# Reworking the first 100 microseconds of a fused Fourier-filter and gated-FFN kernel, and the places of its side work

## The chip, the cores and the metric

The kernel runs on one core of one Trainium2 chip. A core has a matrix engine (PE; PEld is its weight load), a vector engine (DVE), an activation engine (ACT), a GpSimd engine (POOL), and SyncE (SP), which here only issues DMAs. Each engine takes its instructions strictly in program order. DMAs are issued from the queues of SP, ACT and POOL; all of them move their data with the same 16 DMA engines. On-chip data lies in SBUF, matmul results in PSUM.

The metric is the device time of one execution in microseconds. The kernel before has a median of 905.79 us over 10 runs (904.47 to 909.28).

## The reference

`x` has 8 batches of 3,008 tokens with 256 features. Each batch is filtered in frequency space along the tokens, and each filtered token then goes through a gated feed-forward network with 1,536 hidden features.

```python
X = np.fft.rfft(x, axis=1)                      # x: (8, 3008, 256), float32
F = (filt_r + 1j * filt_i)[None, :, :]          # (1505, 256)
y = np.fft.irfft(X * F, n=3008, axis=1)
x2 = y.reshape(24064, 256)
gate = np.maximum(x2 @ w_gate, 0.0)             # w_gate, w_val: (256, 1536)
out = (gate * (x2 @ w_val)) @ w_out             # w_out: (1536, 256)
```

## The kernel before

**Stages.** 3,008 = 94 x 32, so the transform is done as a 94-point and a 32-point part. Per batch there are three stages, all matmuls against small tables.
- Stage A is the 94-point transform. It reads `x` and stores its result to `Abuf` in HBM, from where `at` is loaded with another layout (the exchange goes through HBM). It exists in two forms. The plain form (`items_a`, 16 items, float32 matmuls of 512 columns, L276) is used for batches 0 and 1. The folded form is used from batch 2 on: `load_chunk` loads a quarter of a batch into `XP[j]`, `fold_chunk` adds and subtracts mirrored rows (six tensor_tensor instructions on POOL, L308 to L313), and `tiled_a` does 32 small matmuls (L322), evicts with ACT and DVE (L329) and stores.
- Stage B has six steps per batch. `fwd` (L363) is the 32-point transform into two PSUM tiles `psX`. `product` multiplies them by the real filter `Ftr` and the imaginary filter `Fti` (DVE, L379; in batch 0 some go to POOL by way of a copy `xs` on ACT, L376/L377, chosen by `POOL_U`). `inv` (L393) transforms back, ACT evicts (`dsb`, L400), and SP stores to `Dbuf`.
- Stage C (`item_c`, L448) loads `dC` from `Dbuf`, does the inverse 94-point part and leaves the transposed tokens `yT` of a block of 512: half h=0 is evicted by ACT (L453), half h=1 by DVE (L455).

**The main stream.** 47 blocks of 512 tokens, 12 steps each. A step is `gv` (two matmuls into `psV`, two into `psG`, L464; ACT turns `psV` into `vsb`, L467; DVE makes `prod` = max(psG, 0) * vsb, L469) and `o_part` of the block before (four matmuls into `psO`, L483; output evicted by ACT, L489, at steps 5 and 11). Block 0 has no `o_part` beside it.

**Order.** The order on each engine is the program order, written out by hand. `at_step(s, f)` hangs side work behind step s of the stream (s counts from the first step of block 0): Stages A and B of the next batches, loads, and so on. `end` is the step from which a batch is needed. PSUM is handed out by four tags of two tiles each (`fft`, `psv`, `psg`, `pso`); a tag's tiles are used in turn, and a tile is free when its last reader is done.

**The prologue** runs before the stream: batch 0's `x` and the tables are loaded by SP, the filters by POOL (`load_filters`, after a small copy, `hold_gpsimd`, that waits for the first part of `x`; then `load_own_filters`, the last rows). `warm(n)` issues n matmuls on a constant tile to keep PE busy. `items_a(0)` runs with `warm(1, 256)` or `make_back_t` between its items; `make_back_t`, `make_back_u` build the back-transform tables `I2t`, `I2u` from `F2` (PE, then DVE or ACT); `place_filter` copies filter rows across partitions (L238, DVE, one on ACT). `first_b` is Stage B of batch 0; its `amid` runs items of Stage A of batch 1 between its steps, and the rest of them follow. The loads of `x` of batch 1 wait on SP behind `gate`, a small DMA that reads `at`. The second halves of the gate and value weights (`load_vg`) and the output weight (`load_o`) are issued by POOL after a small load of the end of `Dbuf0`.

Of the kernel before, what the change touches and what calls it, by code (L numbers as in the profile page):

```python
# [12 lines left out]
FP32 = mybir.dt.float32  # L13
# [17 lines left out]
NROW = 96  # L31
# [89 lines left out]
def kernel(  # L121
# [32 lines left out]
    Abuf = [dram.tile([NROW * N2, D], BF16, name=f"Abuf{b}") for b in range(B)]  # L154
    gate = dram.tile([32, 8], BF16, name="gate")
    Dbuf = [dram.tile([NROW * N2, D], BF16, name=f"Dbuf{b}") for b in range(B)]

    XF = [pro.tile([128, NX2 * D], FP32, name=f"XF{c}") for c in range(N2 // NX2)]
    WA = pro.tile([128, NROW], FP32)
# [56 lines left out]
    def load_filters():  # L216

        for src, dst in FILT:
            for a in range(2):
                r, k1, n = a * 64, 1 + 24 * a, NG - 2 * a  # L220
                nc.gpsimd.dma_start(dst[r:r + 31:2, 0:n, :],
                                    _ap(src, k1 * D, [[N1 * D, 16], [1, n * D]]))
                nc.gpsimd.dma_start(dst[r + 1:r + 32:2, 0:n, :],
                                    _ap(src, (N1 - k1) * D, [[N1 * D, 16], [-D, n], [1, D]]))
# [44 lines left out]
    def items_a(b):  # L269

        def one(c, j, st):
            if j == 0:
                st["asb"] = sb.tile([128, NC2 * D], BF16, tag="asb", bufs=4, name="asb")
            psA = ps.tile([128, 512], FP32, tag=fft_tag(True), name="psA")
            o = (c * NC2 % NX2) * D + j * 512
            nc.tensor.matmul(psA[0:NROW], WA, XF[c * NC2 // NX2][:, o:o + 512],  # L276
                             start=True, stop=True)
# [24 lines left out]

    def fold_chunk(b, j):

        xp = XP[j]
        t = fs.tile([128, 2, 512], FP32, tag="fold", bufs=2, name="fold")
        tt = nc.gpsimd.tensor_tensor
        tt(t, xp[:, 0:2], xp[:, 2:4], op=ALU.add)  # L308
# [33 lines left out]

    POOL_U = ((0, 0), (0, 1), (1, 1), (2, 0), (2, 1), (3, 1), (4, 0))
    ats = {}
# [60 lines left out]
    def first_b(amid):  # L405

        cuts = (0, 2, 4, 5, 6)
        for i in range(6):
            fwd(0, i)
            if i > 1:  # L410
                inv(0, i - 2, cuts=cuts)
            for e in range(2):
                product(0, i, e, 0)
                product(0, i, e, 1, pool=(i, e) in POOL_U)
            amid(i)
        inv(0, 4, cuts=cuts)
        inv(0, 5, cuts=cuts)

# [85 lines left out]
    def warm(n, cols=512):  # L504

        psJ = ps.tile([128, 512], FP32, tag=fft_tag(True), name="psJ")
        for i in range(n):
            nc.tensor.matmul(psJ[:, :cols], junk[:, 0:128], junk[:, :cols], start=True, stop=True)

    nc.sync.dma_start(WA, nc.inline_tensor(wa_h, name="dft_wa").ap())  # L510
    q = NX2 * D // 4
    nc.vector.memset(XF[0][:, 0:q], 0.0)
# [14 lines left out]
    load_filters()  # L527
# [19 lines left out]
    warm(18)  # L547
    place_own()
    for half in range(2):
        for a in range(2):  # L550
            place_filter(1, a, half, nc.vector.tensor_copy if a or not half else nc.scalar.copy)
    place_nyq()
# [5 lines left out]
    early = items_a(1)  # L558
# [8 lines left out]
    turn["tags"], turn["side"] = ("fft", "psv", "psg"), "pso"  # L567
# [12 lines left out]
    fs = ctx.enter_context(tc.tile_pool(name="fs", bufs=2))  # L580
    XP = []

    def clear_chunks():
        for i in range(4):
            XP.append(fs.tile([128, 4, 512], FP32, tag=f"XP{i}", bufs=1, name=f"XP{i}"))
            nc.gpsimd.memset(XP[i], 0.0)

    turn["tags"] = ("fft",)
# [4 lines left out]

    for s, z in ((0, 1), (9, 2), (14, 3)):
        at_step(s, lambda z=z: load_d(0, z, z + 1))
    C_AT = (8, 10)
    at_step(2, clear_chunks)
    for b in range(1, B):
        end = (b * S // W - 1) * NFT + C_AT[0] - 5
        if b == 1:  # L600
            for c in range(4):
                at_step(3, lambda c=c: load_at(1, c))
        else:
            for j, e in enumerate((-74, -69, -64, -57)):
                l = end - 113 + NFT * j

# [9 lines left out]
            at_step(end + e + 4, lambda b=b: load_at_tiled(b))  # L616
        for i, l in enumerate((-35, -28, -25, -22, -16, -11, -4) if b == 1 else
                              (-40, -35, -28, -23, -16, -11, -4)):
            if i < 6:
# [3 lines left out]
            if i > 0:  # L623
                at_step(end + l, lambda b=b, i=i: inv(b, i - 1, ("psv", "psg")))
        at_step(end - 2, lambda b=b: load_d(b))
    prev = None
# [41 lines left out]
```

## Time and profile before

| what | value |
|---|---|
| median of 10 runs | 905.79 us |
| the profiled execution | 905.73 us |
| its span in the profile | 903.9 us |
| PE busy | 877.1 us (97%) |
| DVE, ACT, POOL busy | 566.5, 498.5, 359.0 us |
| first matmul of Stage B of batch 0 (L363) | at 33.47 us |
| first matmul of the stream (L464, psV) | at 64.30 us |
| mean granted PE clock | 0.991 |

The span is what the profile shows, and 1.8 us lie around it. PE's busy time is modelled, since matmuls are pipelined: the distance between the starts of instructions is the better measure. The chain that ended last is made of PE for 85% of the span:

```profile
PE 85%; DVE 5%; DMA 4%; ACT 4%; issue 1%; POOL 0%; SPq 0%; DVEq 0%; POOLq 0%
```

### The profile page before, as it was taken

What the parts mean: (1) busy time and instruction counts of PE and PEld (TensorE: products, weight loads), DVE (VectorE), ACT (ScalarE), POOL (GpSimd) and SP (SyncE); (2) the same over time, 40 slices, a digit from 0 to 9 for tenths busy, and PEclk for the clock granted to TensorE, in tenths of its full rate; (3) what the DMA queues carried; (4) which work ended last, traced back from release to release, by engine and by line L of the source; (5) the groups of instructions that cost most, each with busy time, mean ns of one, the idle gap of its engine ahead of it and who ended that gap; (6) DMA issues with size and microseconds to landing.
All of it is one profiled execution on the core that took longest, in us unless ns stands there. A gap on an engine that the chain in (4) does not pass through costs nothing.

```text
span 903.9 us, 19111 instructions
## 1 busy us (share of the span) xinstructions
PE 877.1 (97%) x7096; PEld 512.8 (57%) x7217; DVE 566.5 (63%) x872; ACT 498.5 (55%) x891; POOL 359.0 (40%) x351
## 2 busy tenths in 40 slices
PE   8798899999999999999999999999999999999997
PEld 3334565566555665566655666556655566666665
DVE  2635776577665776657766677657766577655553
ACT  4474556555655556555655465655565555555552
POOL 4342677117680386514763167811768000000000
PEclk9899999999999999999999999999999999999999
DMA  8979337623465343663374533753446512331111
GB/s 249 249 214 227 103 102 176 137 82 110 123 169 121 89 135 115 143 133 113 93 174 115 118 102 98 186 121 93 109 139 153 117 31 83 81 72 36 37 32 50
DMA packets 113662, 109.17 MB, mean 121 GB/s; under 512 B 20290, under 2 KB 98370, under 8 KB 112834
## 3 DMA queue, kind: packets, MB, share of 16 engines
q1 hardware_dynamic: 91078, 81.72, 35.0%
q0 software_dynamic: 22176, 26.01, 11.8%
q8 instruction: 57, 0.93, 0.4%
q10 hardware_dynamic: 316, 0.22, 0.1%
q14 instruction: 35, 0.29, 0.1%
HBM read 61.93 MB, written 49.81 MB: 124 GB/s over the span
## 4 chain that ended last, share of the span: by engine, by line
PE 85%; DVE 5%; DMA 4%; ACT 4%; issue 1%; POOL 0%; SPq 0%; DVEq 0%; POOLq 0%
PE psG L464 25%; PE psO L483 25%; PE psV L464 24%; DVE prod L469 4%; ACT vsb L467 3%; PE psF L322 3%; PE psA L276 3%; PE psD L393 2%; PE psX L363 2%; PE psY L448 1%; DMA WgT<-in_moe_w_gate_dram 1%; DMA XF<-in_x_dram 1%; DMA Abuf<-asb 1%; DMA out_dram<-osb 1%; DMA at<-Abuf 0%
## 5 line engine op out<-in xcount | busy, mean ns | idle before, releaser
L469 DVE SCALAR_TENSOR_TENSOR prod<-psG,vsb 128x512 bf16<-128x512 f32 x564 | 388.9, 690 | 271.5 <-ACT vsb L467 264.7
L467 ACT CAST vsb<-psV 128x512 bf16<-128x512 f32 x564 | 333.0, 590 | 265.7 <-PE psV L464 170.3
L483 PE MATMUL psO<-WoT,prod 128*128 128x256 bf16 x2256 | 336.5, 273 | 1.5
L464 PE MATMUL psG<-yT,WgT 128*128 128x512 bf16 x1099 | 330.0, 380 | 7.3 <-DMA WgT<-in_moe_w_gate_dram 2.4
L464 PE MATMUL psV<-yT,WvT 128*128 128x512 bf16 x1037 | 317.5, 380 | 0.9 <-ACT yT L453 0.6
L483 PEld LDWEIGHTS <-prod 128*128 128x128 bf16 x2256 | 220.7, 98 | 143.3
L464 PEld LDWEIGHTS <-WgT 128*128 128x128 bf16 x1128 | 110.1, 98 | 137.1 <-DMA WgT<-in_moe_w_gate_dram 2.9
L464 PEld LDWEIGHTS <-WvT 128*128 128x128 bf16 x1128 | 98.4, 98 | 42.3 <-issue 31.6
L258 POOL CAST scr<-yT 128x8 f32<-128x8 bf16 x24 | 4.6, 191 | 263.8 <-ACT yT L453 263.8
L379 DVE TENSOR_TENSOR tt<-psX,Ftr 128x512 bf16<-128x512 f32 x96 | 65.0, 681 | 11.9 <-PE psX L363 11.9
L400 ACT CAST dsb<-psD 128x512 bf16<-128x512 f32 x96 | 51.5, 589 | 28.5 <-PE psD L393 28.4
L308 POOL TENSOR_TENSOR fold<-XP 128x1024 f32<-128x1024 f32 x24 | 56.5, 2356 | 25.1 <-PE psF L322 24.9
L489 ACT COPY osb<-psO 128x512 f32<-128x512 f32 x92 | 54.5, 592 | 20.6 <-PE psO L483 20.0
L379 DVE TENSOR_TENSOR uu<-psX,Fti 128x512 bf16<-128x512 f32 x89 | 60.6, 681 | 0.0
L309 POOL TENSOR_TENSOR XP<-XP 128x1024 f32<-128x1024 f32 x24 | 56.4, 2350 | 1.9
L295 POOL DMA_DIRECT2D XP<-in_x_dram x96 | 56.4, 592 | 0.9 <-issue 0.5
L329 DVE CAST asb<-psF 128x512 bf16<-128x512 f32 x48 | 30.9, 686 | 17.3 <-PE psF L322 14.4
L453 ACT CAST yT<-psY 128x512 bf16<-128x512 f32 x47 | 27.5, 586 | 25.1 <-PE psY L448 25.0
L329 ACT CAST asb<-psF 128x512 bf16<-128x512 f32 x48 | 25.8, 589 | 27.2 <-PE psF L322 27.2
L455 DVE CAST yT<-psY 128x512 bf16<-128x512 f32 x47 | 32.0, 681 | 9.3 <-PE psY L448 9.3
L448 PE MATMUL psY<-M,dC 96*128 96x94 bf16 (+18 forms) x604 | 37.5, 199 | 0.0
L276 PE MATMUL psA<-XF,WA 128*96 128x512 f32 x64 | 33.1, 640 | 4.1 <-DMA XF<-in_x_dram 4.1
(66 smaller groups left out, 483.6 us busy)
## 6 DMA issues: line engine op xcount, KB each, us to landing
at<-Abuf SPq DMA_DIRECT2D x32, 384.0 KB
dC<-Dbuf SPq DMA_DIRECT2D x64, 192.0 KB
XP<-in_x_dram POOLq DMA_DIRECT2D x48, 256.0 KB, 5.9
Dbuf<-dsb SPq DMA_DIRECT2D x23, 512.0 KB
XP<-in_x_dram POOLq DMA_DIRECT2D x96, 96.0 KB, 2.7
Abuf<-asb SPq DMA_DIRECT2D x96, 96.0 KB
out_dram<-osb SPq DMA_DIRECT2D x70, 94.0 KB
XF<-in_x_dram SPq DMA_DIRECT2D x18, 256.0 KB
```

The lines of the kernel that those rows point to most:

```text
L276: nc.tensor.matmul(psA[0:NROW], WA, XF[c * NC2 // NX2][:, o:o + 512], start=True, stop=True)
L295: nc.gpsimd.dma_start(xp[r:r + 24, 0:4:2, :], _ap(x, (b * N1 * N2 + o) * D, [[N2 * D, 24], [47 * N2 * D, 2], [1, 512]]))
L308: tt(t, xp[:, 0:2], xp[:, 2:4], op=ALU.add)
L309: tt(xp[:, 2:4], xp[:, 0:2], xp[:, 2:4], op=ALU.subtract)
L329: copy(asf[:, :, q, :], banks[q])
L379: nc.vector.tensor_tensor(p, psX, filt, op=ALU.mult)
L400: nc.scalar.copy(dsb[:, a, o:o + 2, :], psD[a])
L464: nc.tensor.matmul(pt[:, :W], w[:, h, ft * 128:(ft + 1) * 128], yt[:, h, :], start=(h == 0), stop=(h == 1))
L467: nc.scalar.copy(vsb, psV[:, :W])
L469: nc.vector.scalar_tensor_tensor(prod, in0=psG[:, :W], scalar=0.0, in1=vsb, op0=ALU.max, op1=ALU.mult)
L483: nc.tensor.matmul(psO[:, t % 2], prods[ft][:, t * 128:(t + 1) * 128], WoT[:, ft, :], start=(ft == 0), stop=(ft == NFT - 1))
L489: copy(osb[:, t0 % 2:t % 2 + 1], psO[:, t0 % 2:t % 2 + 1])
```

## The change

It does five things.

1. Stage C (but for block 0) takes its PSUM tile from the tags `psv` (h=0) and `psg` (h=1), where it took it from `fft`. The steps of Stage B are 6 steps of the stream apart (5 in batch 1, where they were 3 to 7 apart).
2. `F2` and `tabs` are loaded from ACT's queue at the start, and the first of the filter loads is issued by POOL at once. Batch 0's first piece of `x` is cut in two. There are no more matmuls between the items of Stage A of batch 0. `make_back_t` moves behind all of Stage A and, on DVE, behind the four copies of `Ftr`; then come `make_back_u` and 42 matmuls of `warm` in one piece (36 before, 18 of them between the `make_back_u`).
3. Stage A of batch 1 is no longer plain. `load_pairs` loads its `x` into the same tiles `XF` (now kept for the whole kernel, and viewed as `XP`): eight DMAs on SP directly behind the loads of `at` of batch 0, four on POOL when `at` has landed. Chunks 0 and 1 are folded by DVE, after Stage B of batch 0; chunks 2 and 3 by POOL, the second half of the weights and the output weight being issued between the two. `tiled_a(1, 0)` comes before Stage C of block 0, the other three hang behind steps 1, 3 and 10 of the stream; `at` of batch 1 is loaded behind step 11.
4. `first_b` has six products on POOL (seven before) and `warm` between its steps.
5. The loads of chunk 0 of batch 2 move from step 10 to step 22, those of chunk 1 from step 22 to step 34; chunks 2 (step 34) and 3 (step 46) stay. Stores of the plain Stage A for batches after the first would go to ACT's queue; `items_a` is now called for batch 0 alone.

```diff
-    XF = [pro.tile([128, NX2 * D], FP32, name=f"XF{c}") for c in range(N2 // NX2)]
+    XF = [consts.tile([128, NX2 * D], FP32, name=f"XF{c}") for c in range(N2 // NX2)]
+    XD = [t[:, :].rearrange("p (k n) -> p k n", k=4) for t in XF]
+    XP = [XD[j // 2][:, :, 512 * (j % 2):512 * (j % 2) + 512] for j in range(4)]
...
-                nc.sync.dma_start(_ap(Abuf[b], c * NROW * NC2 * D, [[NC2 * D, NROW], [1, NC2 * D]]),
+                eng = nc.scalar if b and c > 1 else nc.sync
+                eng.dma_start(_ap(Abuf[b], c * NROW * NC2 * D, [[NC2 * D, NROW], [1, NC2 * D]]),
...
-    def fold_chunk(b, j):
+    def load_pairs(b, c, ahead):
+
+        xd = XD[c]
+        if ahead:
+            for q in range(4):
+                r, o = 32 * q, 8 * q + 4 * c
+                nc.sync.dma_start(xd[r:r + 24, 0:4:2, :],
+                                  _ap(x, (b * N1 * N2 + o) * D,
+                                      [[N2 * D, 24], [47 * N2 * D, 2], [1, 1024]]))
+        else:
+            for i in range(2):
+                nc.gpsimd.dma_start(xd[:, 2 * i + 1, :],
+                                    _ap(x, ((b * N1 + 46 + 47 * i) * N2 + 4 * c) * D,
+                                        [[8 * D, 4], [-N2 * D, 32], [1, 1024]]))
+
+    def fold_chunk(b, j, eng=None, pool=None):
...
-        t = fs.tile([128, 2, 512], FP32, tag="fold", bufs=2, name="fold")
-        tt = nc.gpsimd.tensor_tensor
+        t = (pool or sb).tile([128, 2, 512], FP32, tag="fold", bufs=1 if pool else 2, name="fold")
+        tt = (eng or nc.gpsimd).tensor_tensor
...
-    POOL_U = ((0, 0), (0, 1), (1, 1), (2, 0), (2, 1), (3, 1), (4, 0))
+    POOL_U = ((0, 1), (1, 0), (1, 1), (2, 0), (2, 1), (3, 1))
...
-        psY = ps.tile([128, W], FP32, tag=fft_tag(), name="psY")
+        tag = fft_tag() if k == 0 else ("psv", "psg")[h]
+        psY = ps.tile([128, W], FP32, tag=tag, name="psY")
...
+    nc.scalar.dma_start(F2, nc.inline_tensor(f2_h, name="dft_f2").ap())
+    nc.scalar.dma_start(tabs, nc.inline_tensor(tab_h, name="dft_tab").ap())
+    filters = load_filters()
+    next(filters)
...
-    load_x(0, nc.sync, ((0, 0, 2 * q), (0, 2 * q, 4 * q), (1, 0, 2 * q)))
-    nc.sync.dma_start(F2, nc.inline_tensor(f2_h, name="dft_f2").ap())
-    nc.sync.dma_start(tabs, nc.inline_tensor(tab_h, name="dft_tab").ap())
-    load_x(0, nc.sync, ((1, 2 * q, 4 * q),))
+    load_x(0, nc.sync, ((0, 0, q), (0, q, 2 * q), (0, 2 * q, 4 * q), (1, 0, 2 * q), (1, 2 * q, 4 * q)))
...
-        if i >= 13:
-            make_back_t(i - 13)
-        else:
-            warm(1, 256)
...
     for i in range(3):
+        make_back_t(i)
+    for i in range(3):
         make_back_u(i)
+    place_filter(1, 0, 0, nc.vector.tensor_copy)
+    place_filter(1, 1, 0, nc.scalar.copy)
+    place_own()
+    place_filter(1, 0, 1, nc.vector.tensor_copy)
+    place_filter(1, 1, 1, nc.vector.tensor_copy)
+    place_nyq()
+    for i in range(7):
         warm(6)
...
-    nc.sync.dma_start(gate, ats[0][0:32, NG - 1, 0:8])
-    load_x(1, nc.sync, ((0, 0, 2 * q), (0, 2 * q, 4 * q), (1, 0, 4 * q)))
+    for c in range(2):
+        load_pairs(1, c, True)
     hold_gpsimd(ats[0][0:32, NG - 1, 0:8])
+    for c in range(2):
+        load_pairs(1, c, False)
     load_vg(0, DFF // 2)
...
     def amid(i):
-        if i < 2:
-            warm(3, 256)
-        else:
-            for _ in range(2 if i > 2 else 1):
-                next(early)()
+        warm(5 if i < 2 else 4, 256)
...
-    load_d(0, 0, 1)
-    nc.gpsimd.dma_start(pro.tile([1, D], BF16, tag="last", bufs=1, name="last"),
-                        _ap(Dbuf[0], (N2 * NROW - 1) * D, [[D, 1], [1, D]]))
+    load_d(0, 0, 2)
+    for j in range(2):
+        fold_chunk(1, j, nc.vector, None if j else pro)
+    fold_chunk(1, 2)
     load_vg(DFF // 2, DFF)
     load_o()
-    for f in early:
-        f()
+    fold_chunk(1, 3)
+    tiled_a(1, 0)
+    warm(8)
...
-            for c in range(4):
-                at_step(3, lambda c=c: load_at(1, c))
+            for j, e in ((1, 1), (2, 3), (3, 10)):
+                at_step(e, lambda j=j: tiled_a(1, j))
+            at_step(11, lambda: load_at_tiled(1))
...
-                l = end - 113 + NFT * j
+                l = (22, 34, 34, 46)[j] if b == 2 else end - 113 + NFT * j
...
-        for i, l in enumerate((-35, -28, -25, -22, -16, -11, -4) if b == 1 else
-                              (-40, -35, -28, -23, -16, -11, -4)):
+        for i in range(7):
+            l = -33 + 5 * i if b == 1 else -40 + 6 * i
```

More of the change, by code (lines that the diff above doesn't have):

```diff
@@ L154 @@
     Abuf = [dram.tile([NROW * N2, D], BF16, name=f"Abuf{b}") for b in range(B)]
-    gate = dram.tile([32, 8], BF16, name="gate")
     Dbuf = [dram.tile([NROW * N2, D], BF16, name=f"Dbuf{b}") for b in range(B)]
-    XF = [pro.tile([128, NX2 * D], FP32, name=f"XF{c}") for c in range(N2 // NX2)]
+    XF = [consts.tile([128, NX2 * D], FP32, name=f"XF{c}") for c in range(N2 // NX2)]
+    XD = [t[:, :].rearrange("p (k n) -> p k n", k=4) for t in XF]
+    XP = [XD[j // 2][:, :, 512 * (j % 2):512 * (j % 2) + 512] for j in range(4)]
     WA = pro.tile([128, NROW], FP32)
@@ L222, in load_filters @@
                                     _ap(src, k1 * D, [[N1 * D, 16], [1, n * D]]))
+                yield
                 nc.gpsimd.dma_start(dst[r + 1:r + 32:2, 0:n, :],
@@ L416, in first_b @@
         inv(0, 4, cuts=cuts)
+        amid(6)
         inv(0, 5, cuts=cuts)
@@ L508, in warm @@
             nc.tensor.matmul(psJ[:, :cols], junk[:, 0:128], junk[:, :cols], start=True, stop=True)
+    q = NX2 * D // 4
     nc.sync.dma_start(WA, nc.inline_tensor(wa_h, name="dft_wa").ap())
-    q = NX2 * D // 4
+    nc.scalar.dma_start(F2, nc.inline_tensor(f2_h, name="dft_f2").ap())
+    nc.scalar.dma_start(tabs, nc.inline_tensor(tab_h, name="dft_tab").ap())
+    filters = load_filters()
+    next(filters)
     nc.vector.memset(XF[0][:, 0:q], 0.0)
@@ L526 @@
     hold_gpsimd(XF[0][:, 2 * q - 8:2 * q])
-    load_filters()
+    for _ in filters:
+        pass
     load_own_filters()
@@ L544 @@
     for i in range(3):
+        make_back_t(i)
+    for i in range(3):
         make_back_u(i)
-        warm(6)
[L547 to L552, printed above, removed]
+    place_filter(1, 0, 0, nc.vector.tensor_copy)
[5 more added lines that the diff above has]
+    for i in range(7):
+        warm(6)
+    for c in range(2):
+        load_pairs(1, c, True)
     hold_gpsimd(ats[0][0:32, NG - 1, 0:8])
+    for c in range(2):
+        load_pairs(1, c, False)
     load_vg(0, DFF // 2)
-    nc.sync.dma_start(gate, ats[0][0:32, NG - 1, 0:8])
-    load_x(1, nc.sync, ((0, 0, 2 * q), (0, 2 * q, 4 * q), (1, 0, 4 * q)))
-    early = items_a(1)
+    turn["tags"] = ("fft", "psv", "psg")
+    turn["side"] = "pso"
     def amid(i):
-        if i < 2:
-            warm(3, 256)
-        else:
-            for _ in range(2 if i > 2 else 1):
-                next(early)()
-    turn["tags"], turn["side"] = ("fft", "psv", "psg"), "pso"
+        warm(5 if i < 2 else 4, 256)
     first_b(amid)
     turn["tags"], turn["side"] = ("fft", "psv", "psg", "pso"), None
-    load_d(0, 0, 1)
-    nc.gpsimd.dma_start(pro.tile([1, D], BF16, tag="last", bufs=1, name="last"),
-                        _ap(Dbuf[0], (N2 * NROW - 1) * D, [[D, 1], [1, D]]))
+    load_d(0, 0, 2)
+    for j in range(2):
+        fold_chunk(1, j, nc.vector, None if j else pro)
+    fold_chunk(1, 2)
     load_vg(DFF // 2, DFF)
     load_o()
-    for f in early:
-        f()
+    fold_chunk(1, 3)
+    tiled_a(1, 0)
+    warm(8)
     for h in range(2):
@@ L580 @@
     fs = ctx.enter_context(tc.tile_pool(name="fs", bufs=2))
[L581 to L586, printed above, removed]
     turn["tags"] = ("fft",)
@@ L592, in at_step @@
         side.setdefault(s, []).append(f)
-    for s, z in ((0, 1), (9, 2), (14, 3)):
+    for s, z in ((9, 2), (14, 3)):
         at_step(s, lambda z=z: load_d(0, z, z + 1))
     C_AT = (8, 10)
-    at_step(2, clear_chunks)
     for b in range(1, B):
@@ L624 @@
                 at_step(end + l, lambda b=b, i=i: inv(b, i - 1, ("psv", "psg")))
-        at_step(end - 2, lambda b=b: load_d(b))
+        at_step(end - (2 if b > 1 else 1), lambda b=b: load_d(b))
     prev = None
```

## The prediction, written before the changed kernel was run

> **What bounds the kernel now.** I read the page first, then the busy time in short stretches, then PE's, DVE's and POOL's timelines where PE is not full.
>
> ```profile
> span 903.9 us, 19111 instructions
> PE   8798899999999999999999999999999999999997
> POOL 4342677117680386514763167811768000000000
> ```
>
> PE is full from slice 4 on. The stretches show how full, and where not (after the length: busy us of PE, PEld, DVE, ACT, POOL; then granted clock, DMA share, GB/s):
>
> ```profile
> 22.00:24.00 2.00, 2.00 (x35) 0.64 (x34) 1.12 (x4) 0.63 (x2) 0.50 (x1) 1.00 1.17 212
> 40.00:42.00 2.00, 0.00 (x0) 0.00 (x0) 0.00 (x0) 0.40 (x1) 2.00 (x2) 0.50 1.06 338
> 72.00:74.00 2.00, 1.41 (x4) 0.58 (x5) 0.27 (x1) 0.00 (x0) 0.00 (x0) 0.58 1.30 214
> 300.00:400.00 100.00, 99.20 (x852) 58.90 (x865) 66.45 (x103) 57.00 (x104) 50.76 (x45) 1.00 0.49 126
> ```
>
> From about 115 us on PE waits for nothing: the starts of psO's matmuls lie 1.30 us apart in a plain step, 2.18 with a fwd and an inv, 1.53 to 1.56 with a psY, 2.66 with a chunk of Stage A, every time. So neither the even spacing of Stage B nor Stage C's banks can gain there. What can be had lies before 115 us, in PE's timeline:
>
> ```profile
> 27.38 5.34 PE L508 MATMUL psJ<-junk 128*128 128x512 bf16 x24
> 33.47 0.41 PE L363 MATMUL psX<-at,F 64*64 64x256 bf16 x8 [0.75 <-DMA at<-Abuf]
> 42.21 1.99 PE L276 MATMUL psA<-XF,WA 128*96 128x512 f32 x2 [3.85 <-DMA XF<-in_x_dram]
> 64.30 0.59 PE L464 MATMUL psV<-yT,WvT 128*128 128x512 bf16 x2 [0.61 <-ACT yT L453]
> 72.59 1.04 PE L464 MATMUL psG<-yT,WgT 128*128 128x512 bf16 x2 [2.38 <-DMA WgT<-in_moe_w_gate_dram]
> 102.64 0.41 PE L363 MATMUL psX<-at,F 64*64 64x256 bf16 x6 [1.13 <-DVE uu L379]
> ```
>
> The keep-busy matmuls end just as `at` lands; Stage B of batch 0 starts at 33.47, the stream at 64.30; the late gate weights cost a wait and then half clock (two psG matmuls in 1.04 us). The last thing that the change leans on is when the filters land (DVE, POOL and the list of DMA issues):
>
> ```profile
> 28.09 0.95 DVE L238 COPY Ftr<-Ftr 32x3072 bf16<-32x3072 bf16 x1 [0.20 <-DMA Ftr<-in_filt_r_dram]
> 15.80 0.52 POOL L228 DMA_DIRECT2D Ftr<-in_filt_r_dram  x1 [3.01 <-DMA Ftr<-in_filt_r_dram]
> 97.34 2.36 POOL L308 TENSOR_TENSOR fold<-XP 128x1024 f32<-128x1024 f32 x1
> 102.21 1.27 POOL L310 TENSOR_TENSOR XP<-fold 128x512 f32<-128x512 f32 x1
> Ftr<-in_filt_r_dram POOLq DMA_DIRECT2D x1, 16.0 KB, 12.2
> ```
>
> The fourth copy of Ftr had to wait for a load of only 16 KB, issued at 15.80 and landed 12.2 us later, at 28.0. A fold chunk on POOL takes 2.36 + 2.35 + 4 x 1.27, with gaps 10.2 us.
>
> [...]the nearest row, L379 with 512 columns, has 681. [...]2.5 us of idleness before 72.59 brought 3.3 us at half clock.[...]
>
> **The change, part by part.** Its own profiled execution took 905.73 us (span 903.9 and 1.8 around it), 0.06 below the median, so the sum carries over.
>
> *To the start of Stage B.* Before, make_back_t did not wait for a filter. Now DVE copies Ftr four times first, the fourth waits for the 16 KB load, the six copies of I2t follow (0.38 each), make_back_u on PE waits for those, and 42 matmuls stand behind it on PE, in order. The load should land earlier: it no longer waits at 15.80 for an earlier one, one of eight large loads is done beforehand, and the queue's start (first issue at 8.23, first bytes after 12) is paid early. But the four Fti loads still go before it, and the DMA engines are saturated (share 1.17 at 22 to 24 us). I take 24.3, between 22 and 27. From there 0.95 (copy) + 0.8 (two I2t copies) + 1.9 (rest of make_back_u) = 27.9, and 42 x 0.216 = 9.1: Stage B starts at 37.0, though `at` can be there by 32 (Stage A ends about 2 us sooner, fifteen short matmuls of 0.11 being gone). That is 3.5 later than before. If the idle PE ahead of make_back_u drops to half clock, 40; if the load lands at 22, 35.
>
> *Stage B of batch 0.* No Stage A between, no wait for x: DVE has 18 products of 0.61 and about 1.5 of gaps (POOL's six of 1.16 lie beside), so they end 12.5 after the start, where they took 21 before (33.9 to 54.4).
>
> *Folds.* Now DVE folds two chunks, [...]10.4 us, ahead of the evictions of tiled_a(1,0) and of yT in its queue, so the stream waits for them. POOL is through with its products 9.9 after the start and folds chunk 2 at the same time; x is there by then (issued by 35, some 3.7 MB at 340 GB/s as at 40 to 42, about 11 us). If they exclude each other, POOL's two long instructions go first (DVE waits 2.1), then they alternate, and DVE's folds take 2.1 + 10.4 + 4 x 1.27 = 17.6 instead of 10.4. Then two evictions of 0.68 and yT, 2.0. Start of the stream: 37.0 + 12.5 + 17.6 + 2.0 = 69.1, against 64.3: +4.8. The exchange through Dbuf (last eviction 15 after the start, some 6 more) is hidden under that; without the folds it would set the stream's start at about 37 + 22.
>
> *Stream.* Three chunks of Stage A now lie in it: 3 x (2.66 - 1.30) = +4.1. The second half of the weights is issued when POOL has folded chunk 2, about 60.6, and needs some 9 us; step 6 comes 8 after the stream's start, at 77: no wait, -2.5, and no half clock (eight matmuls in 3.27 instead of 1.73), -1.5. Stage B of batch 1 at a spacing of 5 waits no more for DVE: the steps of 3.61 and 3.52 become 2.18, -2.8. One psY wait of 0.4 goes.
>
> *New waits.* Fold of chunk 3 reuses the buffer that tiled_a(1,1) frees at step 1, and ends about 13.3 after the stream's start; PE wants it at 12.5: +0.8 (0 to 2). In batch 2 POOL now does three folds and three loads in a row from step 32 (42.3 us with 3.9 per load) and PE needs the third at step 59, 42.2 us later: +0.7 (0 to 3). psY in psG's tag makes the next psG wait for the product two places before; in the trace prod ends 0.06 before that psG starts: 0 to 2, I take 0.3. `at` of batch 1: from tiled_a to landing took 11.4 in batch 2 (165.6 to about 177), and steps 10 to 18 last 11.6: 0 to 3, I take 0. Together +1.8.
>
> At nothing: loads of batch 2 twelve steps later (POOL only, the folds have their slack counted above); F2 and tabs on ACT's queue (two issues before ACT has work); dC of z=1 earlier (two DMAs); Stage A's stores on ACT's queue, since items_a runs for batch 0 alone, so that this part does nothing.
>
> Sum: +4.8 + 4.1 - 4.0 - 2.8 - 0.4 + 1.8 = +3.5. 905.73 + 3.5 = **909.2 us**.
>
> **Rivals.** (1) *DVE's and POOL's folds run side by side.* Then the stream starts 7.2 earlier, at 61.9: 902.0, faster. Its place is the 18 us after the products, its price the four to six POOL instructions that DVE waits for; it decides for faster as soon as the exclusion costs under 2 us. For it: no row before shows the exclusion. [...] (2) *The filters land early* (16 KB load by 20), so that the 42 matmuls end with `at` at 32.5: 4.5 less, 904.7 with exclusion, 897.5 without. For it: the queue's slow start. Against: 28.0 before and four large loads ahead. (3) *PE is cold at make_back_u*: Stage B at 40, 912. For it: a gap of 3 us in PE's queue, as at 40 to 42.
>
> **How the numbers follow.** This kernel's measurement tells 0.2% (1.8 us) from no change. Chances: forecast 0.40 (its own range 906 to 911.5); rival 3 0.12; rival 1 with Stage B at 37, 0.23; rival 2 with exclusion 0.12, without 0.13. Slower (over 907.6): 0.35 + 0.12 + 0.02 = 0.49. Within: 0.04 + 0.02 + 0.09 = 0.15. Faster (under 904.0): 0.36. The range 898 to 913 leaves out most of rival 2 without exclusion and the end of rival 3.
>
> **What would show it.** L363 first at about 37, behind psJ matmuls, with `at` landed before: the first step. DVE's L326 rows with waits of 1.3 to 2.4 between them that POOL's rows fill: exclusion; rows back to back would refute it. First psV at about 69; no wait on WgT; fwd of batch 1 in steps of 2.18. I am wrong if L363 starts at 33 or DVE's folds take under 12 us, or if a wait for at or a fold inside the stream costs more than 3 us.

## The result, and the profile after

The changed kernel takes 936.22 us (median of 9 runs, 933.83 to 940.73) where the kernel before took 906.27 in the runs beside it: ratio 1.0337, 95% interval 1.0323 to 1.0350. That is 30 us slower; 909.2 us was predicted. The profiled execution took 938.78 us, with a span of 937.0.

The page of the kernel after (the span, then busy tenths of PE and POOL and the granted clock in 40 slices of 23.4 us):

```profile
span 937.0 us, 19362 instructions
PE   7757899799999999999999999999999999999997
POOL 4247229921668048641577028661567100000000
PEclk9876999899999999999999999999999999999999
```

PE is full from the ninth slice on (187 us); before, it was full from the sixth on (113 us). So all of the loss lies in the first 190 us. The busy time in stretches (columns as before: length, then PE, PEld, DVE, ACT, POOL; then clock, DMA share, GB/s) shows where, and that the stream itself has not changed:

```profile
26.00:30.00 4.00, 0.00 (x0) 0.00 (x0) 0.60 (x1) 0.00 (x0) 0.00 (x0) 1.00 1.16 316
48.00:50.00 2.00, 1.40 (x23) 0.80 (x23) 1.05 (x3) 1.39 (x3) 2.00 (x3) 1.00 1.05 162
62.00:66.00 4.00, 0.00 (x0) 0.00 (x0) 2.61 (x3) 0.00 (x0) 0.00 (x0) 0.50 0.88 212
...
178.00:180.00 2.00, 0.00 (x0) 0.00 (x0) 0.00 (x0) 0.00 (x0) 1.92 (x2) 1.00 1.17 151
300.00:400.00 100.00, 99.15 (x838) 59.10 (x851) 67.02 (x103) 57.04 (x103) 47.81 (x49) 1.00 0.46 121
```

At 48 us the DMA engines show as full (a share of 1.05) and move 162 GB/s; in the kernel before they moved 338 at 40 us with a share of 1.06. PE's timeline in the kernel after, with its waits in brackets:

```profile
31.20 1.91 PE L204 MATMUL psI<-I2t,tabs 128*128 128x512 bf16 x3 [5.35 <-DVE I2t L199]
33.75 10.63 PE L528 MATMUL psJ<-junk 128*128 128x512 bf16 x40 [0.22 <-issue]
44.31 0.41 PE L381 MATMUL psX<-at,F 64*64 64x256 bf16 x8
...
66.64 1.03 PE L340 MATMUL psF<-XF,WF 24*32 24x512 f32 x1 [7.27 <-issue]
...
83.82 0.59 PE L484 MATMUL psV<-yT,WvT 128*128 128x512 bf16 x1 [3.90 <-DVE yT L475]
...
115.01 0.41 PE L381 MATMUL psX<-at,F 64*64 64x256 bf16 x6 [3.22 <-DMA at<-Abuf]
...
181.90 0.21 PE L468 MATMUL psY<-M,dC 96*128 96x64 bf16 x1 [5.13 <-DMA dC<-Dbuf]
```

(L381 is `fwd`, L363 before; L484 is `gv`, L464 before; L468 is `item_c`.) Stage B of batch 0 starts at 44.31 instead of 33.47, the stream runs from 83.82 instead of 64.30 (its first matmul starts at 79.55, and the second waits for `yT` until 83.82), and two new waits stand in the stream, for `at` and `dC` of batch 1. After each of these three waits PE runs at half clock for a while (granted clock 0.50 from 84 to 88 us, from 116 to 119 and from 182 to 187, two matmuls of the stream in 1.06 us instead of 0.59): the three steps around the wait for `dC` take 12.4 us where 4.4 would do, 5.13 of it the wait and 2.9 the half clock. Between the stream's start and the first `fwd` of batch 2 the distance grew from 125.68 us (64.30 to 189.98) to 139.86 (83.82 to 223.68): 19.5 us are lost ahead of the stream and 14.2 in it.

What DVE did before the stream, in the kernel after:

```profile
29.40 0.95 DVE L240 COPY Ftr<-Ftr 32x3072 bf16<-32x3072 bf16 x1 [4.29 <-DMA Ftr<-in_filt_r_dram]
...
63.32 1.23 DVE L326 TENSOR_TENSOR fold<-XF 128x1024 f32<-128x1024 f32 x1 [4.64 <-DMA XF<-in_x_dram]
...
66.57 0.69 DVE L329 TENSOR_TENSOR fold<-fold 128x512 f32<-128x512 f32 x1
67.30 2.71 DVE L330 TENSOR_TENSOR fold<-XF 128x512 f32<-128x512 f32 x1
70.05 2.71 DVE L331 TENSOR_TENSOR XF<-XF 128x512 f32<-128x512 f32 x1
```

and POOL beside it:

```profile
66.83 2.62 POOL L326 TENSOR_TENSOR fold<-XF 128x1024 f32<-128x1024 f32 x1 [11.96 <-DMA XF<-in_x_dram]
69.54 2.67 POOL L327 TENSOR_TENSOR XF<-XF 128x1024 f32<-128x1024 f32 x1
```

Three things are to be seen: the last copy of Ftr waits until 29.40; both engines wait for `x` of batch 1; and the same DVE instruction takes 0.69 us until POOL folds too, and 2.71 once it does.

The list of DMA issues says where `x` was. First the kernel after between 30 and 70 us (size of each, us from issue to landing), and the share of POOL's DMA queue, q0, between 48 and 52 us (packets, MB, share of 16 engines):

```profile
XF<-in_x_dram POOLq DMA_DIRECT2D x4, 512.0 KB, 26.5
```

```profile
q0 software_dynamic: 154, 0.63, 104.4%
```

and the queue that carried `x` in the kernel before, between 44 and 48 us:

```profile
q1 hardware_dynamic: 146, 1.56, 93.3%
```

154 packets of 4 KB took 104.4% of 16 engines for 4 us, 434 ns each. In the kernel before, the queue moved 2.5 times as much in the same time: 93 of its 146 packets carried 16 KB and took 615 ns each (48 carried 4 bytes, 5 carried 8 KB). (Packet times below are worked out in this way or taken from the trace's record of each packet.)

### The profile page after: what moved, and what is told of

Same layout as the page of the kernel before. It is cut to its first block, busy times and chain, and to the rows that moved or that the text cites. A ratio compares the mean times of both kernels' runs of the same rounds, so it can differ in the third digit from the quotient of the medians.

```text
span 937.0 us, 19362 instructions
## 1 busy us (share of the span) xinstructions
PE 887.6 (95%) x7215; PEld 513.9 (55%) x7338; DVE 592.1 (63%) x893; ACT 497.0 (53%) x882; POOL 377.5 (40%) x361
## 4 chain that ended last, share of the span: by engine, by line
PE 79%; DMA 9%; DVE 6%; ACT 3%; issue 1%; POOL 1%; SPq 0%; POOLq 0%; DVEq 0%; ACTq 0%
PE psG L484 25%; PE psO L503 23%; PE psV L484 23%; DMA XF<-in_x_dram 4%; DVE prod L489 4%; PE psF L340 3%; ACT vsb L487 3%; PE psD L411 2%; DMA Ftr<-in_filt_r_dram 2%; PE psX L381 2%; PE psY L468 1%; DMA dC<-Dbuf 1%; DMA at<-Abuf 1%; DMA out_dram<-osb 1%; DMA Dbuf<-dsb 1%
## 5 line engine op out<-in xcount | busy, mean ns | idle before, releaser
L484 PE MATMUL psG<-yT,WgT 128*128 128x512 bf16 x1105 | 332.9, 381 | 6.0 <-DVE prod L489 0.3
L484 PE MATMUL psV<-yT,WvT 128*128 128x512 bf16 x1030 | 317.7, 382 | 4.8 <-DVE yT L475 4.3
L484 PEld LDWEIGHTS <-WgT 128*128 128x128 bf16 x1128 | 110.4, 98 | 141.1 <-issue 8.9
L484 PEld LDWEIGHTS <-WvT 128*128 128x128 bf16 x1128 | 98.6, 98 | 44.2 <-issue 33.4
L326 POOL TENSOR_TENSOR fold<-XF 128x1024 f32<-128x1024 f32 x26 | 61.5, 2366 | 40.0 <-PE psF L340 26.9
L418 ACT CAST dsb<-psD 128x512 bf16<-128x512 f32 x96 | 51.5, 589 | 22.1 <-PE psD L411 14.7
L327 POOL TENSOR_TENSOR XF<-XF 128x1024 f32<-128x1024 f32 x26 | 61.4, 2360 | 2.1
L298 POOL DMA_DIRECT2D XF<-in_x_dram x96 | 57.6, 607 | 0.6 <-issue 0.6
L347 ACT CAST asb<-psF 128x512 bf16<-128x512 f32 x56 | 30.2, 589 | 38.4 <-PE psF L340 38.3
L347 DVE CAST asb<-psF 128x512 bf16<-128x512 f32 x56 | 36.1, 686 | 19.3 <-PE psF L340 12.8
L340 PE MATMUL psF<-XF,WF 24*32 24x512 f32 x448 | 39.4, 629 | 8.1 <-issue 7.3
L473 ACT CAST yT<-psY 128x512 bf16<-128x512 f32 x47 | 27.6, 586 | 33.3 <-PE psY L468 33.1
L468 PE MATMUL psY<-M,dC 96*128 96x94 bf16 (+18 forms) x604 | 37.9, 199 | 5.1 <-DMA dC<-Dbuf 5.1
L340 PE MATMUL psF<-fold,WF 24*32 24x512 f32 x448 | 40.9, 631 | 0.8 <-DVE fold L330 0.8
```

Of the source, the lines that this page charges most:

```text
L298: nc.gpsimd.dma_start(xp[r:r + 24, 0:4:2, :], _ap(x, (b * N1 * N2 + o) * D, [[N2 * D, 24], [47 * N2 * D, 2], [1, 512]]))
L327: tt(xp[:, 2:4], xp[:, 0:2], xp[:, 2:4], op=ALU.subtract)
L340: nc.tensor.matmul(banks[q][32 * c:32 * c + 32], WF[r:r + 24, c, :], fold[b, j][c][r:r + 24], start=True, stop=True, tile_position=(r, 32 ...
L347: copy(asf[:, :, q, :], banks[q])
L418: nc.scalar.copy(dsb[:, a, o:o + 2, :], psD[a])
L484: nc.tensor.matmul(pt[:, :W], w[:, h, ft * 128:(ft + 1) * 128], yt[:, h, :], start=(h == 0), stop=(h == 1))
```

## The experiments

All but the runs marked "before" start from the changed kernel.

**Which lateness decides?** Three things are late: the tables (through the filter), `x`, and the folds. e3_back_t takes the filter out of the chain:

```diff
+    for i in range(3):
+        make_back_t(i)
     for half in range(2):
         for a in range(2):
             place_filter(0, a, half, nc.vector.tensor_copy)
-    for i in range(3):
-        make_back_t(i)
```

> The changed kernel with make_back_t directly behind Stage A of batch 0 again, so that the six copies of I2t go ahead of the four copies of Ftr on DVE and make_back_u no longer waits for the filter. Theory (x late is what decides): Stage B of batch 0 starts at 36 to 39 instead of 44.3, but DVE's folds still wait for x until 61 to 63, so the stream starts at most 3 us earlier and the time is 933 to 936. Rival (the late start of Stage B decides): the stream starts 6 to 7 us earlier, at about 77, and the time is 929 to 931.

Measured: 935.1 us. Stage B starts 6.7 us sooner, at 37.59, and DVE's folds still wait for `x`, until 64.85; the stream's second matmul starts at 85.34. From the timelines of PE and DVE in this run:

```profile
37.59 0.41 PE L381 MATMUL psX<-at,F 64*64 64x256 bf16 x8
```

```profile
64.85 1.23 DVE L326 TENSOR_TENSOR fold<-XF 128x1024 f32<-128x1024 f32 x1 [11.85 <-issue]
```

(The profile names nothing for this last wait. By the landings, the second of POOL's loads, which this fold needs, was there at 64.4.) So the late start of Stage B, though 7 us later than predicted, costs nothing while `x` is as late as this: `x` decides. The next run shows that it does cost something once `x` is on time.

**Why is x late?** e2_source changes what is read and leaves the rest (the first pair of lines is SP's loads, each into 24 partitions, the second POOL's, each into 128):

```diff
-                                      [[N2 * D, 24], [47 * N2 * D, 2], [1, 1024]]))
+                                      [[1024, 24], [47 * N2 * D, 2], [1, 1024]]))
...
-                                        [[8 * D, 4], [-N2 * D, 32], [1, 1024]]))
+                                        [[1024, 128], [1, 1024]]))
```

> The changed kernel with the x of batch 1 read from other places: each DMA of load_pairs reads one contiguous block of HBM instead of 4 KB out of every 32 KB (so batch 1 is computed from other tokens); bytes, DMAs, queues and places in SBUF are the same. Theory (source): the rows 32 KB apart are what makes a 4 KB packet of this load take 350 to 490 ns; then the packets take about 170 ns as elsewhere, all of x lands before 54, DVE starts its folds at about 59 instead of 63.3, POOL starts its fold by 58, and the time is 929 to 932. Rival (destination or queue): packets stay above 350 ns, x lands at 63 to 67, and the time stays within 2 us of 936.

Measured: 922.18 us, 14 less, and below what either side expected. POOL's loads land after 12.9 us instead of 26.5. DVE's folds no longer wait for `x`; they start right behind the products:

```profile
57.12 1.96 DVE L326 TENSOR_TENSOR fold<-XF 128x1024 f32<-128x1024 f32 x1
```

What holds the folds here is the late start of Stage B (42.70 in this run). Of the 14 us the earlier stream (74.16 instead of 83.82) is 9.7; the rest lies in the stream, where in this run the wait for `dC` was shorter (2.7 us instead of 5.1) and PE started at full clock (the first two `psG` matmuls in 0.59 us instead of 1.06). But SP's packets did not gain: 0.62 MB between 36 and 40 us, as in the changed kernel (0.61). So the two queues are slow for two reasons. e7_place writes SP's to other partitions:

```diff
-                nc.sync.dma_start(xd[r:r + 24, 0:4:2, :],
+                nc.sync.dma_start(xd[q:q + 93:4, 0:4:2, :],
```

> The changed kernel with the eight DMAs of load_pairs on SP writing to every fourth partition instead of 24 neighbouring ones (so batch 1 is folded from wrongly placed rows); source, bytes and queues are the same. Theory (place): with the source in one block these packets still took 320 ns, so it is the 24 neighbouring partitions that hold them up; now they take about 170 to 220 ns, the loads on POOL's queue get going 3 to 4 us sooner, x lands at 59 to 63, and the time is 931 to 934. Rival (source alone, or the number of rows per DMA): they keep 320 to 350 ns, and the time stays within 2 us of 936.

Measured: 934.69 us. SP's queue moves 0.64 MB in 3 us (35 to 38; 159 ns for the typical packet) instead of 0.61 in 4 (36 to 40; 309 ns): the place was what held it up. Once POOL's loads run, every packet takes 440 to 500 ns again, and they land after 25.2 us. For POOL's loads, then, I tried larger pieces (e8_wide: `XF` as one tile, 8 KB of every 32 in one piece, two DMAs on POOL's queue instead of four), the order of the rows (e9_ascending: `N2 * D` for `-N2 * D`, from row 15) and their distance (e10_rows28: `-28 * D`).

> The changed kernel with XF as one tile and its view XP laid out so that load_pairs fetches 8 KB in one piece out of every 32 KB of x (four DMAs on SP, two on POOL) instead of 4 KB (eight and four); the same bytes. Theory (width of the source's pieces): an 8 KB packet takes 320 to 350 ns as in the plain loads of the kernel before, x lands before 50, and the time is 918 to 923, as with the source in one block. Rival (the reversed or strided rows themselves): a packet takes 700 ns or more, x lands at 60 or later, and the time is 933 to 937.

> The changed kernel with the four loads of mirrored rows on POOL's queue reading the same rows of x in rising instead of falling order (so mirrored rows meet the wrong partners); bytes, queue and places are the same. Theory A (distance): it is the 32 KB between neighbouring rows of the source that slows these loads; packets stay at 430 to 500 ns once they run, x lands at 63 to 67, and the time is 933 to 938. Theory B (falling order): the order is what slows them; packets take 160 to 240 ns, x lands before 54, and the time is 920 to 927.

> The changed kernel with the four loads of mirrored rows on POOL's queue reading rows 28 KB apart instead of 32 KB, in falling order as before (so batch 1 is folded from other tokens); bytes, queue and places are the same. Theory A (distance of 32 KB): packets take 160 to 240 ns, x lands before 54, and the time is 920 to 927. Theory B (falling order): packets stay at 430 to 500 ns, x lands at 63 to 67, and the time is 933 to 938.

Size, order and distance are none of them the cause: e8_wide took 950.0 us, with 46.3 us from issue to landing, worse than either theory had it; e9_ascending 937.22 (26.3 us), e10_rows28 935.01 (26.1 us). What e2_source had changed besides was the form of the pattern: two dimensions instead of three. e13_runs4 has three dimensions and a source that is nearly one block, e14_rows128 two and a scattered source; e15_places keeps the scattered rows and writes to every fourth partition. The line of e13_runs4 comes first, then that of e14_rows128:

```diff
-                                        [[8 * D, 4], [-N2 * D, 32], [1, 1024]]))
+                                        [[33 * 1024, 4], [1024, 32], [1, 1024]]))
+                                        [[N2 * D, 128], [1, 1024]]))
```

> The changed kernel with each of the four loads on POOL's queue reading four blocks of 128 KB with a gap of 4 KB between them, instead of 4 times 32 rows far apart (so batch 1 is folded from other tokens); the access pattern keeps its three dimensions, places, bytes and queue are the same. Theory A (scattered rows): packets take 160 to 250 ns once SP's loads are through, x lands by 55, and the time is 922 to 930. Theory B (a source in more than one run is handed out to the DMA engines in another way[...]): packets stay at 430 to 500 ns, and the time is 933 to 938.

> The changed kernel with each of the four loads on POOL's queue reading 128 rows of x in rising order, 4 KB out of every 32 KB, in a pattern of two dimensions (so batch 1 is folded from other tokens); places, bytes and queue are the same. Theory A (scattered rows): packets stay at 430 to 500 ns, and the time is 933 to 938. Theory B (the way a pattern of three dimensions is handed out): packets take 160 to 250 ns, and the time is 922 to 930.

> The changed kernel with all of x of batch 1 written to every fourth partition: the loads on SP as in the run that did this for them alone, and each load on POOL's queue cut into four of 32 rows, in rising order (so batch 1 is folded from wrongly placed rows); the source rows and the bytes are those of the change. Theory A (scattered rows of the source slow POOL's loads, wherever they are written): packets on POOL's queue stay at 400 ns or more, x lands at 58 or later, and the time is 930 to 938. Theory B (neighbouring partitions slow them, as they do SP's): packets take 160 to 250 ns, x lands by 54, and the time is 922 to 929.

The DMA issues between 30 and 70 us, first of e13_runs4, then of e14_rows128:

```profile
XF<-in_x_dram POOLq DMA_DIRECT2D x4, 512.0 KB, 26.0
```

```profile
XF<-in_x_dram POOLq DMA_DIRECT2D x4, 512.0 KB, 12.0
```

e13_runs4 took 937.89 us, e14_rows128 925.87. Both write the same partitions from the same queue. So for POOL's loads it is the form of the pattern that costs, not the rows in HBM, and for SP's it is the place (e7_place). e15_places took 927.73 (POOL issues its 16 DMAs until 48, and PE waits 7.8 us for a product behind them; from 38 to 50 the packets took 196 to 239 ns on average). It changes POOL's form and place together, so it doesn't tell which of them helped.

How the form and the place act is not shown by any run; what they cost is. SP's queue moved 153 GB/s into 24 neighbouring partitions (changed kernel, 36 to 40 us) and 213 into every fourth (e7_place, 35 to 38). POOL's queue moved 158 with the three-dimensional loads (changed kernel, 48 to 52) and 283 with the two-dimensional ones (e14_rows128, 44 to 48).

How many DMA engines work on one load can be estimated, because the trace has the time of each of the 16 increments of a DMA's semaphore. Of POOL's first load in the changed kernel, 12 increments were there 12.6 us after its issue and the last 4 came at 26.3 to 26.6; of the second load 8 and 8, of the third 4 and 12. In e14_rows128 all 16 of the first load were there after 11.0. In e8_wide, which has two such loads, the DMA engines were busy to 4 to 6 tenths in every slice from 63 to 81 us, about half of the 16. From the increments, which come by fours, and from this half, my estimate is four engines to a load. With the four loads under way the engines show as full in the slow form as in the fast one: the share of POOL's queue was 104.4% in the changed kernel (48 to 52 us) and 96.3% in e14_rows128 (44 to 48). So what grew is the time of a packet (434 ns against 159), and why a packet takes longer no record tells. A form of these loads that is right and fast was not tried.

**Was it to be seen before?** Yes. `load_chunk` in the kernel before has two loads of the very form of POOL's, at half the width, and they stand in its list of DMA issues:

```profile
XP<-in_x_dram POOLq DMA_DIRECT2D x48, 256.0 KB, 5.9
```

Two of them (0.5 MB), issued at 95.92 and 96.62, had landed at 102.9. That is 75 GB/s, less than a quarter of the 340 that the prediction took from the plain loads.

**Do the folds exclude each other?** e4_hold:

```diff
-    fold_chunk(1, 2)
     load_vg(DFF // 2, DFF)
     load_o()
+    hold_gpsimd(fold[1, 1][3][:, 504:512])
+    fold_chunk(1, 2)
```

> The changed kernel with POOL's fold of chunk 2 behind the end of DVE's two folds (a small copy on POOL reads DVE's last result) and the loads of the second half of the weights ahead of it, so that POOL and DVE never fold at the same time. Theory (exclusion): DVE's folds take 10.4 to 11 us instead of 18.6, the stream starts 7 to 8 us earlier, at about 76; POOL's fold of chunk 2 then ends at about 84 and its chunk of Stage A behind step 3 waits some 3 to 5 us for it, the one behind step 10 some 1 to 3; together 2 to 5 us faster, 931 to 934. Rival (DVE's folds are slow by themselves, or by DMA traffic into the same memory): they still take 16 us or more, the stream starts no earlier, and the time is 940 or more.

Measured: 935.22 us. DVE's folds take 10.7 us (61.78 to 72.47) instead of 18.6, each instruction 0.69, 1.22 or 1.23 again; that the two engines' folds hold each other up is shown. The stream starts only 2.6 us sooner all the same, at 81.23, because of another wait on PE:

```profile
79.95 1.03 PE L468 MATMUL psY<-M,dC 96*128 96x94 bf16 x12 [7.04 <-DMA dC<-Dbuf]
```

The exchange through `Dbuf`, behind `x` and the weights in the DMA engines, is what comes next in this run. A part of that is the edit's own, since it issues 0.8 MB of weights ahead of the folds.

**Whence the wait for dC of batch 1?** e1_table undoes the shift of batch 2's loads:

```diff
-                l = (22, 34, 34, 46)[j] if b == 2 else end - 113 + NFT * j
+                l = end - 113 + NFT * j
```

> The changed kernel with one line undone: the loads of x of batch 2 stand at steps 10, 22, 34 and 46 of the stream again (22, 34, 34, 46 in the change). Theory (backlog): the two chunks at step 34 make POOL late, so that it issues the fourth chunk at 167 instead of at its step (about 160), just ahead of the loads of dC of batch 1, which then take 12 us; without the backlog the wait of 5.13 us for dC at 176 goes, with the half clock behind it: 8.0 us in all, and the time is 927 to 930. Rival (late store): the wait comes from Dbuf being stored and dC being loaded one step later than before (spacing 5 in Stage B of batch 1); then the wait for dC stays above 4 us and the time at 934 to 937.

Measured: 933.51 us, 2.7 less by the medians; the profiled span is 931.2, 5.8 shorter. The wait for `dC` is gone, so it was the backlog: POOL issues the fourth chunk at 160.13 instead of 167.34, clear of the loads of `dC`, which land in 3.0 to 6.6 us where most of them had taken 12. In the ten other runs that keep the shifted loads PE waits 2.7 to 6.3 us at this place. But only a part of the 8 us was gained. PE's list of waits in this run (total, times, longest):

```profile
PE psX L381 <- DMA at<-Abuf: 6.2, 2, 3.6
```

The first chunk's loads now start at 98 and run into the exchange of `at`, whose wait grows from 3.2 to 6.2 us, and the half clock with it. Moving these loads later had taken them out of one exchange and put them into the next.

**Parts alone, on the kernel before.** e5_even has part 1 of the change and nothing else (to part 1 belongs that `dC` of batch 1 is loaded one step later); e6_even_vg adds `hold_gpsimd(XF[1][:, 4 * q - 8:4 * q])` in the place of the small load of the end of `Dbuf0`, and has Stage B and `dC` of batch 1 one step earlier; e11_even_split is e5_even and loads the second halves of the weights in two pieces, `load_vg(768, 1024)` and `load_vg(1024, 1536)`, at the old place.

> The kernel before with part 1 of the change alone: Stage C of every block but the first in the tags psv and psg, Stage B of batch 1 at a spacing of 5, of the others at 6, dC of batch 1 loaded one step later. Theory: the steps of 3.61 and 3.52 us at 101 and 107 become 2.18 and one wait of 0.4 goes, nothing else moves: 3 us faster than before, 902.5 to 904. Rival: what the change moves there brings waits of its own (dC of batch 1 late by the later store, psG behind Stage C): 905 to 909.

> The kernel before with part 1 of the change (Stage B of batch 1 from one step earlier on, so that dC is loaded where it was), and with the second halves of the weights issued by POOL as soon as x of batch 1 has landed, at about 52, instead of behind the last of Dbuf at 60. Theory: the wait of 2.4 us for WgT at 72 and the half clock behind it go as well: 7 us faster than before, 898 to 901. Rival (contention): the 0.8 MB of weights delay the stores and loads of Dbuf, Abuf and dC between 52 and 64, the stream starts 2 to 4 us later, and the time is 902 to 905.

> The kernel before with part 1 of the change alone (0.9956 of before), and the second halves of the weights loaded in two pieces, columns 768 to 1023 of both first, then the rest, at the same place in POOL's queue. Theory: step 6 needs the first third only, which lands some 4 us sooner; the wait of 2.3 us for WgT at 71 goes and what little clock was lost with it, and the rest is there for step 8: 2 to 3 us faster than without the split, 900 to 901.5. Rival: the pieces of 512 bytes take as long as the whole did, or step 8 waits instead of step 6: 902.5 to 905.

e5_even: 902.96 us against 907.01, ratio 0.9956 (0.9943 to 0.9969). This part is a gain, and the kernel with it alone beats both the kernel before and the changed one. e6_even_vg: 908.82 against 907.01, ratio 1.0019 (0.9994 to 1.0044), so 6 us worse than e5_even, which has the weights at their old place: the wait for WgT is gone, and the exchange ahead of the stream pays. PE in that run:

```profile
70.36 1.03 PE L449 MATMUL psY<-M,dC 96*128 96x94 bf16 x12 [6.94 <-DMA dC<-Dbuf]
```

The small load that was removed had kept 0.8 MB of weights out of the exchange: the loads of `dC` are issued at 66.31, and at 58.15 in e5_even. e11_even_split: 905.28 against 906.51, ratio 0.9984 (0.9974 to 0.9994), worse than without the split; a wait for WgT of 1.9 us stays, and one of 2.5 for `dC` stands where e5_even had one of 1.1.

**Does the sum hold once x is quick?** e12_mended puts four edits together: the source of POOL's loads of e2_source, the place of e7_place, the order of e3_back_t, and `(21, 22, 34, 46)` for batch 2's loads.

> The changed kernel with four things at once: the mirrored rows on POOL's queue from one block of HBM, the eight loads on SP's queue to every fourth partition (both make batch 1 wrong, and take the slowness out of its load), make_back_t ahead of the copies of Ftr, and the loads of x of batch 2 at steps 21, 22, 34 and 46. The exclusion of the folds and the three chunks in the stream stay. Theory: then the terms of the prediction hold: Stage B of batch 0 at 37 to 38, DVE's folds from 51 on in 15 to 18 us, the stream at 68 to 71, no wait for dC at 176, a wait of 3 to 5 us for at; 910 to 915. Rival (something else is still in the way, such as the stores and loads of Dbuf behind x): the stream starts at 74 or later, and the time is 918 or more.

Measured: 915.57 us against 906.51, ratio 1.0099 (1.0074 to 1.0124). PE's timeline of this run:

```profile
36.41 0.41 PE L381 MATMUL psX<-at,F 64*64 64x256 bf16 x8
...
69.98 0.38 PE L484 MATMUL psV<-yT,WvT 128*128 128x512 bf16 x1 [0.57 <-DVE yT L475]
...
98.30 0.55 PE L381 MATMUL psX<-at,F 64*64 64x256 bf16 x6 [2.57 <-DMA at<-Abuf]
```

The stream starts at 70.0, where 69.1 was predicted, and nothing waits for `dC`. So of the 30 us some 20 belong to the slow load, the backlog and the filter together; how they share the 20 no run tells. Even without them this plan is slower than the kernel before: the stream starts 5.7 us later, has three chunks of Stage A in it, and waits for `at`. That wait costs 4.5 us with its half clock, and is most of what is left between 915.57 and the predicted 909.2. Why `at` is late was not tried; it is late here with `x` on time.

## Why the prediction was wrong, point by point

- **"x is there by then (issued by 35, some 3.7 MB at 340 GB/s as at 40 to 42, about 11 us)" is the step that failed.** The rate came from plain loads with another pattern, and the pattern of the new ones was not priced, though loads of that form stood in the trace. POOL's loads took 26.5 us and landed at 63 to 67, where the folds were to start at 49.5. With POOL's half of it mended (e2_source) the stream starts 9.7 us sooner, at 74.16; with SP's half as well and the filter out of the chain (e12_mended) 13.8 us sooner, at 70.0.
- **Start of Stage B, 37.0: mis-sized, and hidden behind `x`.** The 16 KB load landed at 29.3, not 24.3, 15.7 us after its issue at 13.59; the matmuls behind it took 10.63 us for 40 at a reduced clock (0.82 on average), not 9.1 for 42. Stage B started at 44.31; 5.0 of the 7.3 us are the load's. Rival 2, filters early, is refuted, and the cold PE of rival 3 was there. e3_back_t shows that the lateness cost nothing behind the slow `x`. Without the slow `x` it counts: the folds start right behind the products, at 57.12 in e2_source and at 49.61 in e12_mended, where Stage B starts 6.3 us sooner. Why the load took so long was not tried.
- **Stage B of batch 0, 12.5 us:** 13.9 (44.76 to 58.69).
- **Folds with exclusion, 17.6 us:** nearly right in its size, 18.6, and 10.7 without POOL beside them, where the sum had 10.4. No row of before showed that the folds would hold each other up; rival 1, folds side by side, is refuted by e4_hold. What one fold instruction takes on DVE was not shown before either (0.69 us with 512 columns and 1.23 with 1,024 here). The order was another one: DVE did four of its instructions before POOL began, because POOL's `x` came later still. Last fold to stream: 1.9 (2.0 predicted).
- **"The exchange through Dbuf ... is hidden": right where the folds are long.** In e12_mended nothing waits for it. In e4_hold, with short folds, a slow `x` and weights moved ahead, it ended last, and PE waited 7.04 us.
- **Stream: three chunks, the wait for WgT, the even steps.** PE doesn't wait for WgT any more, as predicted. e12_mended needs 17.12 us from the stream's start to its first `psO` matmul, 16.33 before: +0.8, where +0.1 was predicted for chunks, weights and their half clock. In the changed kernel it is +3.0, because the stream starts on a cold PE after the wait of 3.90 (two `psG` matmuls in 1.06 us, 0.59 in e12_mended); this was not in the sum. The even steps gained less than the -2.8 predicted: between the first `psO` and the first `fwd` of batch 2, e5_even is 2.1 us shorter than the kernel before, since the steps behind the two waits grew. The rest of its 4.0 us lies elsewhere; 1.3 of it is an earlier start of the stream, which the edit doesn't touch.
- **The small new waits, 0.8, 0.7 and 0.3:** none above 0.3 us stands in PE's list of waits; the larger waits for `yT`, `at` and `dC` may hide them.
- **"at of batch 1, 0 to 3, I take 0":** the wait is 3.22 us, and 5.2 with the half clock behind it, from the distances of steps. So this wait cost PE 2 us more than itself. It is not the slow load's doing: e12_mended has 2.57.
- **Batch 2's loads "at nothing, POOL only":** 8.0 us (wait 5.13, half clock the rest). They made POOL 7 us late with the fourth chunk, and so put its loads onto the loads of `dC` in the DMA engines.
- **The edit of the plain Stage A's stores** does nothing, as predicted.

The rise of 33.1 us in span: 19.5 ahead of the stream, 3.0 in its first 12 steps, 5.2 for `at`, 8.0 for `dC`, -2.1 for the even steps; that is 33.6, and the -0.5 left lies behind the first `fwd` of batch 2. In these terms the prediction had +4.8 ahead of the stream, and the 14.7 us beyond it are more than half of its miss.

## What to carry to other kernels

Price a new DMA by its own pattern, and look first for a load of the same form in the trace that you have. What to compare, by these runs, is the number of dimensions of its source (26.0 us from issue to landing with three in e13_runs4, 12.0 with two in e14_rows128) and the partitions that it writes (309 ns for the typical packet into 24 neighbouring ones, 159 into every fourth in e7_place). A rate taken from another pattern in the same trace can be off by more than a factor of two (340 GB/s taken, 158 found). Time that a load needs can also be time that it takes from an exchange in flight (in e1_table the wait for `at` went from 3.2 to 6.2 us), so ask of each load that is moved which exchange it lands on, not only which engine issues it. And take a large change apart: one of its parts was a gain of 4 us, hidden under a loss of 34.

## What the runs showed of the hardware that was not expected

- A 4 KB packet of these loads took 159 ns in the fast form (e14_rows128, 48 to 52 us), and 434 to 541 on average in the slow one (changed kernel, 44 to 60). The share of the DMA engines alone did not tell the slow loads from the quick ones; share and GB/s must be read together (1.05 with 162 GB/s against 1.06 with 338).
- The slow loads slowed their neighbours: packets of 1.5 KB of the weights took 286 ns beside POOL's loads of `x` in the changed kernel (52 to 60 us) and 135 in e2_source; SP's packets in e7_place went from 159 ns to 480 when POOL's began.
- Folding at the same time slowed both engines: POOL's short folds went from 1.27 to 1.59 and 2.13 us while DVE's went from 0.69 to 1.64 and 2.71.
